# Order of issue inside the slots of a fused FFT-mixing and MLP kernel, and first weight sums in earlier tiles

## The chip, the cores and the metric

One Trainium2 chip, one core of it. The metric is the device time in microseconds of one execution of the whole kernel: a LayerNorm, a 2-D FFT filter with its inverse and a residual, then a LayerNorm, a two-layer MLP with relu and a second residual, all in one program.

The names of engines in the profile: PE is the matrix engine (PEld its weight loads, which overlap its matmuls), DVE the vector engine, ACT the scalar engine, POOL the GpSimd engine, SP the engine whose queue issues the DMAs. PSUM is the memory into which PE writes; POOL cannot reach it.

## The reference

```python
def _A_ref(x, w_r, w_i):
    B, S, D = x.shape
    X = jnp.fft.rfft2(x, axes=(-2, -1)) * (w_r + 1j * w_i)
    return jnp.fft.irfft2(X, s=(S, D), axes=(-2, -1))

def _B_ref(x, w1, w2):
    h = jnp.maximum(jnp.einsum("bsd,df->bsf", x, w1), 0)
    return jnp.einsum("bsf,fd->bsd", h, w2)

h = x + _A_ref(layernorm(x), w_r, w_i)       # x: 1 x 2048 x 576
out = h + _B_ref(layernorm(h), w1, w2)       # w1: 576 x 4608, w2: 4608 x 576
```

All data are float32. The output is `out`.

## The kernel before

**Stages.** The forward transform (L296 on) and the middle of the filter (L340 on) are matmuls with constant tables. Then x is loaded a second time (sixteen DMAs, L377) and a loop over `t` (L641) runs the inverse transform in 16 tiles of 128 rows: `inv_d(t)` makes y (its second half by one POOL subtraction, L396), `inv_a(t-1)` one tile later multiplies y and adds it to x, which gives h in the tile `A`. Two tiles behind that follow the statistics of the second LayerNorm (`stat2`), its application by ACT (`norm2`, two tiles of rows at a time, as a generator that is advanced at the end of each turn of the loop) and `project`, which transposes the normalised rows into `T`.

**The MLP** is cut in 18 blocks `s` (nine blocks of 512 hidden columns, for each half of the rows), and each block is two-level: both layers are computed by a seven-product scheme of Strassen's kind with 2 x 2 blocks. That is why sums of blocks appear on all sides: sums of normalised rows (L419 to L422, POOL), sums of w1 blocks (`sums1`, POOL, L480 to L485), sums of w2 blocks (`sums2`, POOL, L501: T1 to T4), sums of hidden blocks (`hsum`, DVE, L520: S1 to S4). Every float32 operand of a matmul is split in a high and a low part: ACT copies it to a rounded type (L161), DVE subtracts the copy from the operand (L467), and three matmuls (high x high, high x low, low x high) replace one. Such pairs are `split1` (w1, four groups 0 to 3 of the tile `WF`), `split2` (w2 blocks) and `form` (hidden blocks, in the buffers that the profile calls HF, G and one of the e tiles).

**Order.** A unit `S` is 14 slots `k` (`slot`, L626). Slot `k` holds the first-layer product `mm1` of block `S` (six or eight matmuls of 512 columns, L543), its evacuation `evac` (copies and relu by ACT; in three of seven slots a DVE addition, L556, and then the relu of its result by ACT, L557), the second-layer product `prod` of block `S-1` (twelve matmuls of 288 columns, L569) with the DVE addition of its PSUM result into `A` (L574), and small tasks: `tasks_old` for block S-1 and `tasks_new` for block S. `form(S-1, k+2)` prepares the hidden operand of the product two slots on. Unit 0 has no second layer and is spread over turns 16 to 22 of the loop over `t`, two slots a turn, among the last tiles' statistics and transposes; units 1 to 17 have both layers; unit 18 has only the second.

Nothing reorders this: each engine runs its instructions in the order in which the program text issues them, and waits on semaphores where an operand or a buffer is not ready. The order written out by hand is thus the order of every queue, SP's and POOL's too.

Buffers that matter here: `WF` exists once, so a group of it is rewritten only after the last first-layer product that reads it; `V2` keeps each w2 block and its sums in place; hidden operands rotate through four buffers, w2 operands through four (`VF`); products with odd number up to 11 share one PSUM tile (`c1`), and each waits for the addition into `A` of the one before; `X` and `Y` are the two PSUM banks of the first layer. The pool `e` has ten buffers, given out in the order in which they come free; the two w1 blocks (`V1`) and their sums (`SW`) take three of them for good.

The order of products and where their operands come from:

```python
PRODS = "P1a P2a P1b P2b P6a P5a P6b P3a P7a P5b P7b P3b P4a P4b"   # slots 0 to 13
# P1: A11 x B11; P2: A12 x B21; P6: S2 x T2; P5: S1 x T1; P3: S4 x B22; P7: S3 x T3; P4: A22 x T4
ORDER = A11, A12, S2, S1, S3, A22, S4     # first layer, slots 0 to 6 and again 7 to 13
```

Group 0 of `WF` holds A11 and A12, group 1 A22, group 2 S1 and S2, group 3 S3 and S4.

Of the kernel before, what the change touches and what calls it, by code (L numbers as in the profile page):

```python
# [18 lines left out]
NT = 16  # L19
# [105 lines left out]
def kernel(ctx: ExitStack, tc: tile.TileContext, x, w_r, w_i, w1, w2, cc2, c1, fb, ib, c3, out):  # L125
    nc = tc.nc
# [26 lines left out]
    def ebuf(shape, dt=F32):  # L153
        e = sb([128, EW], "e", EB, dt, "e")[:, :int(np.prod(shape[1:]))]
        return e.rearrange("p (a b) -> p a b", a=shape[1]) if len(shape) == 3 else e
# [258 lines left out]
    def norm2(t0):  # L414
        z = ebuf([128, 2, D])
        yield from ln_apply(xs, t0, 2, stats.pop(t0), [z[:, i, :] for i in range(2)])
        S = ebuf([128, 4, 256])
        b11, b21, b12, b22 = z[:, 0, :256], z[:, 0, 256:512], z[:, 1, :256], z[:, 1, 256:512]
        nc.gpsimd.tensor_sub(S[:, 0], b12, b11)  # L419
        nc.gpsimd.tensor_sub(S[:, 2], b22, b12)  # L420
        nc.gpsimd.tensor_sub(S[:, 1], b22, S[:, 0])
        nc.gpsimd.tensor_sub(S[:, 3], b21, S[:, 1])  # L422
        Zs[t0 // 2] = z, S

    def project(i, part):
        P, q = i // 4, slice(128 * (i % 4), 128 * (i % 4) + 128)
# [45 lines left out]
        for h in range(2):  # L472
            nc.sync.dma_start(t[64 * h:64 * h + 64, 4], w1[512:576, f])

    def sums1(v, part):
        t, S = V1[v % 2], M["SW"]
        A11, A12, A21, A22 = (t[:, 2 * k:2 * k + 2, 128 * f:128 * f + 128] for f, k in ((0, 0), (0, 1), (1, 0), (1, 1)))
        S1, S2, S3, S4 = (S[:, 2 * i:2 * i + 2] for i in range(4))
        if part == 0:
            nc.gpsimd.tensor_add(S1, A21, A22)  # L480
            nc.gpsimd.tensor_sub(S2, S1, A11)
        else:
            nc.gpsimd.tensor_sub(S3, A11, A21)
            nc.gpsimd.tensor_sub(S4, A12, S2)
            nc.gpsimd.tensor_sub(S[:, 8], t[:, 4, :128], t[:, 4, 128:])  # L485

    def split1(v, g):
        t, S = V1[v % 2], M["SW"]
# [19 lines left out]
    def split2(s, n_):  # L508
        f = vform(s, n_)
        split(f[:, 0], f[:, 1], V2[PLACE.get(n_, n_)])  # L510
# [6 lines left out]
    def hsum(s, n_, j=slice(0, 2)):  # L517
        d, a, b, f = {"S3": ("S3", "A11", "A21", nc.vector.tensor_sub), "S1": ("A21", "A21", "A22", nc.vector.tensor_add),
                      "S2": ("A11", "A21", "A11", nc.vector.tensor_sub), "S4": ("A12", "A12", "A11", nc.vector.tensor_sub)}[n_]
        f(raw(s, d, j), raw(s, a, j), raw(s, b, j))  # L520
# [58 lines left out]
    def tasks_old(s, k):  # L579
        if k == 0:  # L580
            hsum(s, "S1", 0)
            hsum(s, "S2", 1)
        if k == 1:
            hsum(s, "S2", 0)
        if k in (2, 3):
            split2(s, ("T2", "T1")[k - 2])
            hsum(s, "S4", k - 2)
        if k == 5:
            split2(s, "B22")
            split2(s, "T3")  # L590
        if k == 8:
            split2(s, "T4")

    def tasks_new(s, k):
        u, m = divmod(k, 7)
        v = 2 * s + u
        if v and k == 7:
            split1(v, 1)
        if v and k in (1, 7):
            split1(v, 3)  # L600
        if m == 0 and v + 2 < 2 * NS:
            load1(v + 2)
        if v + 1 < 2 * NS:
            if m in (1, 2):
                sums1(v + 1, m - 1)
            if k in (4, 6, 10, 12, 13):
                split1(v + 1, {4: 0, 6: 2, 10: 0, 12: 2, 13: 1}[k])
        if s:
            for kk, n_ in ((4, "B11"), (5, "B22"), (6, "B12"), (9, "B21")):
                if k == kk:  # L610
                    load2(s, n_)
        if k == 9:
            hsum(s, "S3")
        if k == 11:
            split2(s, "B11")
            sums2("T1", "T3", "T2")
        if k == 12:
            hsum(s, "S1", 1)
        if k == 13:
            split2(s, "B21")  # L620
            sums2("T4")
        if s == 8 and u == 1:
            b = ORDER[m][1]
            nc.sync.dma_start(T[:, b].rearrange("p h k n -> p (h k n)").bitcast(F32), Td[b].rearrange("p a i n -> p (a i n)"))

    def slot(S, k):  # L626
        if S < NS:
            mm1(S, *divmod(k, 7))
            evac(S, *divmod(k, 7))
            if k >= 12:  # L630
                form(S, k - 12)
        if S:
            if k < 12:
                form(S - 1, k + 2)
            prod(S - 1, k)
            tasks_old(S - 1, k)
        if S < NS:
            tasks_new(S, k)

    gen = None  # L640
    for t in range(NT + 7):  # L641
        if t < NT:
            inv_d(t)
        if t == NT - 1:
            pools.pop("x").release()
            newpool("mid", "left")
        if t == 8:
            V1.append(ebuf([128, 5, 256]))
            M["SW"] = ebuf([128, 9, 128])
            load1(0)  # L650
        if t == 10:
            sums1(0, 0)
            sums1(0, 1)
        if t == 12:
            split1(0, 0)
            split1(0, 1)
        if t == 14:
            split1(0, 2)
            split1(0, 3)
        if t == 16:  # L660
            V1.append(ebuf([128, 5, 256]))
            load1(1)
            M.update((n_, sb([128, 512], n_, pool="mid")) for n_ in ("s1", "u2", "u3"))
            pools.pop("pd").release()
            newpool("pxy", "left", space=PSUM)
            M["XY"] = [pools["pxy"].tile([128, 512], F32, tag=n_, name=n_, bufs=1) for n_ in "XY"]
            HF.append(sb([128, 2, 2, 256], "HF", 1, F32R, "mid"))
            V2["T2"] = sb([128, 2, 288], "T2", pool="mid")
        if t == 18:
            for h in ("1", "2"):  # L670
                vv = ebuf([128, 2, 576]).rearrange("p a (j d) -> p a j d", j=2)
                for k in range(2):
                    V2["B" + h + "12"[k]] = vv[:, k]
                    load2(0, "B" + h + "12"[k])
        if t == 20:
            VF.append(ebuf([128, 1152], F32R).rearrange("p (a j d) -> p a j d", a=2, j=2))
        if t == 21:
            VF.append(ebuf([128, 1152], F32R).rearrange("p (a j d) -> p a j d", a=2, j=2))
            HF.append(ebuf([128, 1024], F32R).rearrange("p (a j d) -> p a j d", a=2, j=2))
        if t % 2 == 1 and 5 <= t <= NT + 3:  # L680
            gen = norm2(t - 5)
            next(gen)
        if 0 <= t - 3 < NT:
            stat2(t - 3)
        if 0 <= t - 1 < NT:
            inv_a(t - 1)
        if t >= NT:
            slot(0, 2 * (t - NT))
            slot(0, 2 * (t - NT) + 1)
        if t >= 7:  # L690
            project(*divmod(t - 7, 2))
        if gen:
            next(gen, None)
    for _ in range(2):
        VF.append(ebuf([128, 1152], F32R).rearrange("p (a j d) -> p a j d", a=2, j=2))
    G = sb([128, 2, 1024], "G", 1, F32R, "mid").rearrange("p b (a j d) -> p b a j d", a=2, j=2)
# [29 lines left out]
```

## Time and profile before

| | |
|---|---|
| median of 3 runs | 1084.51 us (1083.0 to 1086.38) |
| the profiled execution | 1083.62 us, span of its instructions 1081.8 us |
| PE busy | 1014.2 us, 94% of the span |
| DVE busy | 883.8 us, 82% |
| ACT, POOL busy | 513.0 us, 357.5 us |
| granted PE clock | 0.995 |
| inverse, from its first tile to the first slot of unit 0 | about 117 to 188 us |
| unit 0 | 188 to 227 us |
| units 1 to 17 | 227 to 1048 us |
| unit 18 and the last stores | 1048 to 1082 us |

How to read the lines of the profile. A line of the timeline is: start in us, busy time of the line's instructions, engine, line of the kernel, operation, output <- inputs by the program's names (buffer numbers left out), shape, how many; in square brackets the idle time just before it and what ended it. A line of waits is: who waited, for whom, microseconds in total, times, the longest. The chain of waits is followed back from the last instruction. A helper records under its own line: L161 is every ACT copy, L467 every subtraction of a split, so the tile's name tells which one is meant (`WF` a w1 split; `e<-e,e` with 576 columns a w2 split; `G`, `HF` or `e<-h,e` with 512 columns a form). Matmuls are pipelined, so that their durations overlap: distances between starts say what a matmul costs.

### The profile page before, as it was taken

The numbers are of one execution on the slowest core, as the hardware profiler recorded it, in microseconds if no ns is written. First come the engines' busy times: TensorE is split into PE (matmuls) and PEld (weight loads), VectorE is DVE, ScalarE is ACT, GpSimd is POOL, SyncE is SP. The second block draws the span as 40 slices with busy tenths as digits, with TensorE's granted clock in tenths as the row PEclk, the third lists the DMA queues.
The fourth block names the chain that finished last, engine by engine and source line by source line (L and its number), as shares of the span: only waits on it lengthen the run. The fifth ranks groups of instructions, "written<-read, shape, count | busy, mean of one in ns | idle before, by whom it ended". The sixth has DMA issues, their size and how long they took to land.

```text
span 1081.8 us, 16681 instructions
## 1 busy us (share of the span) xinstructions
PE 1014.2 (94%) x6344; PEld 884.3 (82%) x6344; DVE 883.8 (82%) x1367; ACT 513.0 (47%) x904; POOL 357.5 (33%) x384
## 2 busy tenths in 40 slices
PE   8999987789999999999999999999999999999997
PEld 7788775668898888889898888888888888888886
DVE  7587788668888888888888888888888888888887
ACT  4533244555454544545445444545445454445443
POOL 4200265542423334241423333241432424142320
PEclk9999998999999999999999999999999999999999
DMA  8840800842021222112111834202111211212003
GB/s 240 197 126 4 198 1 9 261 144 69 25 69 36 58 58 61 58 36 68 36 58 50 321 85 114 69 25 69 36 58 58 61 58 36 69 34 60 16 29 88
DMA packets 73935, 85.12 MB, mean 79 GB/s; under 512 B 5248, under 2 KB 69248, under 8 KB 72960
## 3 DMA queue, kind: packets, MB, share of 16 engines
q1 hardware_dynamic: 73856, 84.06, 27.1%
q8 instruction: 50, 0.82, 0.3%
q14 instruction: 29, 0.24, 0.1%
HBM read 71.98 MB, written 12.06 MB: 78 GB/s over the span
## 4 chain that ended last, share of the span: by engine, by line
DVE 59%; PE 12%; ACT 12%; issue 12%; DMA 2%; POOL 2%; DVEq 0%; SPq 0%; ACTq 0%; POOLq 0%
DVE A L574 14%; DVE h L520 10%; DVE e L467 9%; DVE WF L467 8%; PE d L158 7%; DVE h L556 6%; DVE G L467 5%; ACT h L557 4%; ACT G L161 3%; DVE HF L467 3%; PE dd L158 2%; ACT HF L161 2%; ACT e L161 1%; PE d L569 1%; DMA e<-in_B_w_dram 1%
## 5 line engine op out<-in xcount | busy, mean ns | idle before, releaser
L569 PE MATMUL d<-e,G 128*128 128x288 f32 x1512 | 226.3, 296 | 19.3 <-DVE e L467 16.1
L569 PEld LDWEIGHTS d<-e,G 128*128 128x128 f32 x1512 | 212.5, 188 | 38.3 <-DVE e L467 21.3
L557 ACT ACTIVATE h<-h 128x512 f32<-128x512 f32 x108 | 68.3, 632 | 367.4 <-DVE h L556 367.0
L543 PE MATMUL X<-T,WF 128*128 128x512 f32 x864 | 225.9, 397 | 4.4 <-ACT u L161 3.3
L574 DVE TENSOR_TENSOR A<-A,d 128x576 f32<-128x576 f32 x252 | 188.3, 747 | 1.8 <-PE d L569 1.8
L543 PEld LDWEIGHTS X<-T,WF 128*128 128x128 f32 x864 | 155.2, 189 | 32.0 <-ACT u L161 4.0
L543 PE MATMUL Y<-T,WF 128*128 128x512 f32 x648 | 168.3, 395 | 3.8 <-DVE h L556 3.8
L467 DVE TENSOR_TENSOR G<-h,G 128x512 fp32r<-128x512 f32 x126 | 87.6, 695 | 65.3 <-ACT G L161 65.1
L520 DVE TENSOR_TENSOR h<-h,h 128x512 f32<-128x512 f32 (+1 forms) x126 | 137.5, 1102 | 0.0
L543 PEld LDWEIGHTS Y<-T,WF 128*128 128x128 f32 x648 | 115.8, 188 | 24.0 <-DVE h L556 4.5
L569 PE MATMUL d<-e,e 128*128 128x288 f32 x756 | 113.9, 297 | 13.3 <-DVE e L467 9.8
L569 PEld LDWEIGHTS d<-e,e 128*128 128x128 f32 x756 | 105.9, 188 | 24.6 <-DVE e L467 11.9
L467 DVE TENSOR_TENSOR WF<-e,WF 128x640 fp32r<-128x640 f32 (+2 forms) x144 | 121.9, 858 | 3.2 <-ACT WF L161 3.2
L569 PE MATMUL d<-e,HF 128*128 128x288 f32 x756 | 113.0, 296 | 4.8 <-DVE e L467 4.7
L569 PEld LDWEIGHTS d<-e,HF 128*128 128x128 f32 x756 | 106.7, 188 | 12.9 <-DVE e L467 7.7
L480 POOL TENSOR_TENSOR e<-e 128x256 f32<-128x256 f32 x36 | 40.2, 1117 | 218.1 <-DVE WF L467 215.3
L501 POOL TENSOR_TENSOR e<-e 128x576 f32<-128x576 f32 x18 | 32.3, 1796 | 192.8 <-DVE e L467 192.8
L161 ACT ACTIVATE WF<-e 128x640 fp32r<-128x640 f32 (+2 forms) x144 | 90.8, 644 | 0.0
L161 ACT ACTIVATE G<-h 128x512 fp32r<-128x512 f32 x126 | 77.9, 619 | 16.1 <-DVE h L520 14.0
L467 DVE TENSOR_TENSOR e<-e,e 128x576 fp32r<-128x576 f32 x108 | 79.7, 752 | 1.3 <-ACT e L161 1.3
L161 ACT ACTIVATE e<-e 128x576 fp32r<-128x576 f32 x108 | 70.6, 670 | 0.0
L467 DVE TENSOR_TENSOR HF<-h,HF 128x512 fp32r<-128x512 f32 x63 | 44.2, 702 | 31.9 <-ACT HF L161 31.7
(108 smaller groups left out, 1343.5 us busy)
## 6 DMA issues: line engine op xcount, KB each, us to landing
e<-in_B_w_dram SPq DMA_DIRECT2D x72, 288.0 KB, 2.9
e<-in_B_w_dram SPq DMA_DIRECT2D x36, 512.0 KB, 3.8
Td<-h SPq DMA_DIRECT2D x28, 256.0 KB, 3.1
T<-Td SPq DMA_DIRECT2D x7, 1024.0 KB, 10.4
A<-in_A_x_dram SPq DMA_DIRECT2D x16, 288.0 KB, 9.1
e<-in_B_w_dram SPq DMA_DIRECT2D x72, 64.0 KB, 3.5
out_dram<-A SPq DMA_DIRECT2D x32, 144.0 KB, 2.5
X<-in_A_x_dram SPq DMA_DIRECT2D x12, 288.0 KB, 7.6
```

The costliest lines, as they stand in the source:

```text
L158: nc.tensor.matmul(o, l, r, start=start, stop=stop)
L161: nc.scalar.activation(o, i, AF.Copy, **kw)
L467: nc.vector.tensor_sub(l, v, h)
L480: nc.gpsimd.tensor_add(S1, A21, A22)
L501: nc.gpsimd.tensor_sub(d, a, b)
L520: f(raw(s, d, j), raw(s, a, j), raw(s, b, j))
L543: nc.tensor.matmul(o, l, r, start=first and n_ == 0, stop=n_ == len(ops) - 1, skip_group_check=not first)
L556: nc.vector.tensor_add(h, a, Y)
L557: nc.scalar.activation(h, h, AF.Relu)
L569: nc.tensor.matmul(o[:, tt], f[:, l, j, 128 * tt:128 * tt + 128], w[:, r, j], start=first and n_ == 0, stop=n_ == 5, skip_group_check=not ...
L574: nc.vector.tensor_add(xt, xt, o)
```

## The change

In a slot, `form(S-1, k+2)` now comes first, ahead of the first-layer product and its evacuation (and `form(S, k-12)` in slots 12 and 13). Inside the unit, tasks move: the split of T2 from slot 2 to slot 1; the split of B21 from slot 13 to slot 12; the sum T4 from slot 13 to slot 4 of the next unit, and T2's sum ahead of T3's; half of S1 from slot 12 to slot 13; in slots 9 to 13 the hidden sums and w2 splits come ahead of the w1 tasks; the split of w1's group 3 from slot 1 to slot 2; the two parts of the w1 sums from slots 1, 2, 8, 9 to slots 3, 5, 9, 12.

In the inverse, the buffers and loads of the first two w1 blocks move from turns 8 and 16 to turns 0 and 2, the sums of block 0 from turn 10 to turns 0 and 1, those of block 1 from unit 0 to turns 4 and 5, and the splits of block 0 from turns 12 and 14 to turns 2, 3 and 4. The four POOL sums of the normalised rows are no longer part of the generator: a function `sumsx` issues two of them at the end of one turn and two at the end of the next.

```diff
     def norm2(t0):
         z = ebuf([128, 2, D])
         yield from ln_apply(xs, t0, 2, stats.pop(t0), [z[:, i, :] for i in range(2)])
-        S = ebuf([128, 4, 256])
+        Zs[t0 // 2] = z, ebuf([128, 4, 256])
+
+    def sumsx(i, part):
+        z, S = Zs[i]
         b11, b21, b12, b22 = z[:, 0, :256], z[:, 0, 256:512], z[:, 1, :256], z[:, 1, 256:512]
-        nc.gpsimd.tensor_sub(S[:, 0], b12, b11)
-        nc.gpsimd.tensor_sub(S[:, 2], b22, b12)
-        nc.gpsimd.tensor_sub(S[:, 1], b22, S[:, 0])
-        nc.gpsimd.tensor_sub(S[:, 3], b21, S[:, 1])
-        Zs[t0 // 2] = z, S
+        for d, a, b in (((0, b12, b11), (2, b22, b12)), ((1, b22, S[:, 0]), (3, b21, S[:, 1])))[part]:
+            nc.gpsimd.tensor_sub(S[:, d], a, b)
...
-    def sums1(v, part):
+    def sums1(v, part, only=None):
...
+        ops = ((S1, A21, A22), (S2, S1, A11), (S3, A11, A21), (S4, A12, S2), (S[:, 8], t[:, 4, :128], t[:, 4, 128:]))
+        for n_ in ((0, 1), (2, 3, 4))[part] if only is None else [only]:
+            (nc.gpsimd.tensor_sub if n_ else nc.gpsimd.tensor_add)(*ops[n_])
...
         if k == 1:
             hsum(s, "S2", 0)
-        if k in (2, 3):
-            split2(s, ("T2", "T1")[k - 2])
-            hsum(s, "S4", k - 2)
+            split2(s, "T2")
+        if k == 2:
+            hsum(s, "S4", 0)
+        if k == 3:
+            split2(s, "T1")
+            hsum(s, "S4", 1)
+        if k == 4:
+            sums2("T4")
...
     def tasks_new(s, k):
         u, m = divmod(k, 7)
         v = 2 * s + u
+        if k == 9:
+            hsum(s, "S3")
+        if k == 11:
+            split2(s, "B11")
+            sums2("T1", "T2", "T3")
+        if k == 12:
+            split2(s, "B21")
+        if k == 13:
+            hsum(s, "S1", 1)
         if v and k == 7:
             split1(v, 1)
-        if v and k in (1, 7):
+        if v and k in (2, 7):
             split1(v, 3)
...
-            if m in (1, 2):
-                sums1(v + 1, m - 1)
+            if v and k in (3, 5, 9, 12):
+                sums1(v + 1, int(k in (5, 12)))
...
-        if k == 9:
-            hsum(s, "S3")
-        if k == 11:
-            split2(s, "B11")
-            sums2("T1", "T3", "T2")
-        if k == 12:
-            hsum(s, "S1", 1)
-        if k == 13:
-            split2(s, "B21")
-            sums2("T4")
...
     def slot(S, k):
+        if S and k < 12:
+            form(S - 1, k + 2)
         if S < NS:
+            if k >= 12:
+                form(S, k - 12)
             mm1(S, *divmod(k, 7))
             evac(S, *divmod(k, 7))
-            if k >= 12:
-                form(S, k - 12)
         if S:
-            if k < 12:
-                form(S - 1, k + 2)
             prod(S - 1, k)
             tasks_old(S - 1, k)
...
-        if t == 8:
+        if t in (0, 2):
             V1.append(ebuf([128, 5, 256]))
+            load1(t // 2)
+        if t == 0:
             M["SW"] = ebuf([128, 9, 128])
-            load1(0)
-        if t == 10:
-            sums1(0, 0)
-            sums1(0, 1)
-        if t == 12:
-            split1(0, 0)
-            split1(0, 1)
-        if t == 14:
-            split1(0, 2)
-            split1(0, 3)
+        if t in (0, 1, 4, 5):
+            sums1(t // 4, t % 4)
+        if t in (2, 3, 4):
+            for g in ((2,), (3, 0), (1,))[t - 2]:
+                split1(0, g)
         if t == 16:
-            V1.append(ebuf([128, 5, 256]))
-            load1(1)
...
         if gen:
             next(gen, None)
+        if 6 <= t < NT + 6:
+            sumsx(*divmod(t - 6, 2))
```

More of the change, by code (lines that the diff above doesn't have):

```diff
@@ L478, in sums1 @@
         S1, S2, S3, S4 = (S[:, 2 * i:2 * i + 2] for i in range(4))
[L479 to L485, printed above, removed]
+        ops = ((S1, A21, A22), (S2, S1, A11), (S3, A11, A21), (S4, A12, S2), (S[:, 8], t[:, 4, :128], t[:, 4, 128:]))
+        for n_ in ((0, 1), (2, 3, 4))[part] if only is None else [only]:
+            (nc.gpsimd.tensor_sub if n_ else nc.gpsimd.tensor_add)(*ops[n_])
     def split1(v, g):
```

## The prediction

> **What bounds the kernel now.** I read the busy shares by stretch first, then the chain of waits, then one steady unit in the timeline. Columns of a stretch: length, busy time of PE, PE's weight loads, DVE, ACT, POOL, then granted clock, DMA share, GB/s.
>
> ```profile
> 277.10:325.28 48.18, 46.22 (x270) 41.12 (x270) 40.77 (x58) 23.69 (x43) 16.29 (x15) 1.00 0.18 53
> 126.98:183.19 56.21, 47.45 (x267) 38.58 (x265) 48.64 (x100) 23.65 (x38) 33.72 (x57) 0.97 0.06 16
> ```
>
> ```profile
> 614.41 1.84 DVE h L520
> ...
> 662.58 1.84 DVE h L520
> ```
>
> The chain comes back to the same DVE addition every 48.17 us: that is one unit, and there are 17 with both layers in them (S=1 to 17). PE's 46.22 hides the waits, since modelled ends overlap; starts show them:
>
> ```profile
> 566.17 1.56 PE L543 MATMUL X<-T,WF 128*128 128x512 f32 x6
> 567.57 1.75 PE L569 MATMUL d<-e,G 128*128 128x288 f32 x12
> 569.15 1.56 PE L543 MATMUL Y<-T,WF 128*128 128x512 f32 x6
> ...
> 571.01 0.30 PE L569 MATMUL d<-e,G 128*128 128x288 f32 x1
> 572.42 1.73 PE L569 MATMUL d<-e,G 128*128 128x288 f32 x11 [1.12 <-DVE e L467]
> ...
> 579.28 1.83 PE L569 MATMUL d<-e,e 128*128 128x288 f32 x12 [0.29 <-DVE A L574]
> ...
> 583.16 1.73 PE L569 MATMUL d<-e,G 128*128 128x288 f32 x11 [0.53 <-DVE e L467]
> ```
>
> Six first-layer matmuls take 1.40 from start to start (566.17 to 567.57), eight 1.86 (569.15 to 571.01), twelve second-layer ones 1.58. A unit has 100 and 168 of them: 100 x 0.232 + 168 x 0.1325 = 45.46. So 48.18 - 45.46 = 2.72 us per unit are waits, all on DVE: product 1 for the split of B21, product 3 for the sum of product 1, product 4 for the split of T2. The unit's waits say why DVE is late:
>
> ```profile
> DVE G L467 <- ACT G L161: 3.7, 3, 1.3
> DVE e L467 <- ACT e L161: 2.4, 2, 1.2
> DVE HF L467 <- ACT HF L161: 1.2, 1, 1.2
> PE d L569 <- DVE e L467: 1.6, 2, 1.1
> PE d L569 <- DVE A L574: 0.3, 1, 0.3
> ```
>
> Six times DVE adds u+Y (L556), ACT does the relu and only then the copy of the form, and DVE, whose next work is that form's subtraction, stands 1.22 us: 7.3 us. 40.8 busy + 7.3 = 48.1: DVE is full.
>
> **The change: forms first.** The form's copy and subtraction now stand ahead of the addition, so nothing on DVE follows a relu directly. The six waits go (-7.3 us of DVE per unit). If that were all, PE would stream at 45.46. But POOL moves too, and it costs DVE time:
>
> ```profile
> 562.36 0.75 DVE L574 TENSOR_TENSOR A<-A,d 128x576 f32<-128x576 f32 x1
> 563.03 0.75 DVE L467 TENSOR_TENSOR e<-e,e 128x576 fp32r<-128x576 f32 x1
> 563.70 0.69 DVE L467 TENSOR_TENSOR G<-h,G 128x512 fp32r<-128x512 f32 x1
> 564.30 0.75 DVE L574 TENSOR_TENSOR A<-A,d 128x576 f32<-128x576 f32 x1
> 564.96 1.25 DVE L467 TENSOR_TENSOR WF<-e,WF 128x512 fp32r<-128x512 f32 x1
> 566.14 1.92 DVE L520 TENSOR_TENSOR h<-h,h 128x512 f32<-128x512 f32 x1
> 567.98 0.67 DVE L556 TENSOR_TENSOR h<-u,Y 128x512 f32<-128x512 f32 x1
> ...
> 579.65 0.82 DVE L467 TENSOR_TENSOR WF<-e,WF 128x640 fp32r<-128x640 f32 x1
> 580.49 0.69 DVE L467 TENSOR_TENSOR G<-h,G 128x512 fp32r<-128x512 f32 x1
> ```
>
> ```profile
> 563.86 1.81 POOL L501 TENSOR_TENSOR e<-e 128x576 f32<-128x576 f32 x1 [10.29 <-DVE e L467]
> 565.75 1.76 POOL L501 TENSOR_TENSOR e<-e,e 128x576 f32<-128x576 f32 x1
> ...
> 580.55 1.25 POOL L483 TENSOR_TENSOR e<-e 128x256 f32<-128x256 f32 x1 [3.99 <-DVE WF L467]
> ```
>
> Starts give the free pitches: 0.66 for A, 0.67 for a w2 split, 0.60 for a 512-wide one. Against POOL they take turns: POOL's first T ends 565.67, and the WF subtraction from 564.96 hands on only at 566.14, 0.47 later; the second T ends 567.51, and the hidden sum from 566.14 hands on at 567.98, again 0.47. POOL in turn ends 1.30 after the DVE operation that held it (566.21 to 567.51), a w1 sum 0.62 after (581.18 to 581.80). A, which reads PSUM, keeps 0.66 beside POOL.
>
> The Trainium skill, page "SBUF — State Buffer", section "Who interferes with whom", calls this an exclusive lock for DVE instructions with two SBUF inputs against GpSimd ones that read SBUF. The trace agrees (0.47 after 565.67 and after 567.51). By that rule the new POOL order costs PE a wait; without it the sum would be the first rival's.
>
> POOL's queue after product 12 is now T1, T2, T3, then the second part of the w1 sums (slot 12), its first part (slot 3), T4 (slot 4). Their inputs are there, so POOL runs them in one go; before, T4 and the sums waited on splits. I lay DVE's order against that, with 0 where product 12 hands PE on. PE would hand on product 13 at 3.45, 0 at 6.43, 1 at 9.88, 2 at 12.86, 3 at 16.31 (1.39 or 1.86 for the first layer, 1.59 for the product). T1 starts behind form 0's subtraction and ends at 0.4; T2, free, takes 1.4 (1.30 and a start) and ends at 1.9. DVE, with the moment at which it hands on ("sum k" adds product k into A, L574; "addition" is L556; "half of S" an L520 sum of hidden blocks):
> sum 12 0.86; B21's split, held by T2, 1.9 + 0.54 = 2.43 (T3 then ends 2.51 + 1.30 = 3.81); WF group 2, held by T3, 4.28 (first w1 sum 4.96); form 1 5.43 (second 6.11); addition 13 6.03; sum 13 6.69 (third, short, meanwhile); half of S1 7.29 (fourth 7.97); group 1 8.31 (fifth 8.99); form 2 9.46 (T4 10.84); sum 0 10.12; the other half of S1, held by T4, 11.31; half of S2 11.91; form 3 12.51; addition 1 13.11; sum 1 13.77; half of S2 14.37; T2's split, whose copy follows the relu of addition 1, 15.19; form 4 15.79; sum 2 16.45; half of S4 17.05; WF group 3 (now slot 2, was slot 1; 0.74 free, from 579.65 on without the short sum's hold) 17.79, its result 0.08 later. Then:
> - Product 1 needs B21 at 6.43 + 1.86 = 8.29, has it at 2.5: its wait goes. Product 3 needs sum 1 at 14.7, has it at 13.9. Product 4 has T2 in time. So all three old waits go.
> - New: the third matmul of slot 4 needs group 3's low half at 16.31 + 0.46 = 16.77 and gets it at 17.93: **1.16 us of wait**. From there DVE regains PE by slot 9 and the unit closes.
> Unit: 45.46 + 1.16 = 46.6, a gain of 1.55 to 1.6; over 17 units -27. Bounds: no wait, -2.72 each; two sums changing turns puts it 0.7 later, and half as much again, -0.8 each: -14 to -46.
>
> **First tiles.** The load of the first w1 block moves from tile 8 to tile 0 on SP, behind the sixteen x loads; its POOL sums from tile 10 to tiles 0 and 1, ahead of the y subtraction (L396) of tile 1.
>
> ```profile
> 106.54 13.04 SPq L170 DMA_DIRECT2D A<-in_A_x_dram  x16
> ```
>
> ```profile
> A<-in_A_x_dram SPq DMA_DIRECT2D x16, 288.0 KB, 9.1
> ```
>
> ```profile
> 107.00:128.00 21.00, 19.66 (x168) 16.34 (x165) 12.71 (x26) 4.13 (x8) 2.65 (x3) 1.00 0.97 225
> ```
>
> ```profile
> 123.40 1.13 PE L158 MATMUL dd<-e,cc 128*128 128x288 f32 x4
> ...
> 167.10 3.58 PE L158 MATMUL d<-e,X 128*128 128x290 f32 x12
> ```
>
> ```profile
> 126.98 0.46 DVE L393 TENSOR_TENSOR e<-e,d 128x288 f32<-128x288 f32 x1 [0.77 <-ACT e L161]
> ...
> 166.08 1.78 DVE L467 TENSOR_TENSOR WF<-e,WF 128x640 fp32r<-128x640 f32 x2
> ...
> 171.24 0.46 DVE L393 TENSOR_TENSOR e<-e,d 128x288 f32<-128x288 f32 x1 [0.65 <-POOL e L419]
> ...
> 178.63 1.92 DVE L467 TENSOR_TENSOR WF<-e,WF 128x512 fp32r<-128x512 f32 x2
> ...
> 192.73 0.69 DVE L556 TENSOR_TENSOR h<-s,Y 128x512 f32<-128x512 f32 x1 [1.96 <-PE Y L543]
> ```
>
> The DMA engines are 97% busy to 128; the last x load, issued at 119, lands 9.1 later. 512 KB behind it at 225 GB/s need 2.3, and the landing some 0.7: about 131. POOL stands until then, adds twice (0.7 each, the free time of a 256-wide sum: 1.25 at 580.55 less the 0.55 in which DVE's form held it) and makes tile 1's y by 133.2. PE, whose order has tile 1's second half in the matmuls at 123.40, stands behind it from 124.0 to 133.3. After 3.7 idle, tile 13's matmuls took 3.58 at 167.10; I take that for tile 3, so DVE's L393 of tile 3 comes at 138.0, 11.0 after 126.98. From there DVE sets the pace (48.64 busy of 56.21). Splits of groups 3, 0 and 1 now lie in tiles 3 and 4 (0.74, 0.74, 0.47: +1.95); those at 166.08 and 178.63 go (-1.7, -1.85) and so does the 0.65 at 171.24. PE, no longer late, removes the 1.96 at 192.73. Sum: 11.0 + 1.95 - 3.55 - 0.65 - 1.96 = +6.8; take **+6.5**, bounds +2 (the load at 129, the clock up) to +10 (nothing regained).
>
> The page "DMA: Bandwidth & Descriptors" of the Trainium skill, section "Two DMAs through the same engine are not ordered", lets descriptors of one queue start in order, though they finish out of it; it speaks against the change. In the trace the x loads' 9.1 fit a line that is waited in; no row shows one overtaken.
>
> **The small edits.** The four normalised-tile sums (sumsx) go out in pairs a tile apart: PE's waits for POOL there shrink, but DVE sets the pace, so I count 0, and up to -3 if DVE were not the cover. SP issues nothing urgent behind the early loads: 0. ACT's form copies stand ahead of the X copies that release a bank; by the walk the copy after slot 4's X ends 0.8 before slot 5 needs it: 0, and 0.5 a unit if ACT is later. The last unit:
>
> ```profile
> 1051.49 1.73 PE L569 MATMUL d<-e,G 128*128 128x288 f32 x11 [1.59 <-DVE e L467]
> ```
>
> B21's wait of 1.59 goes there; with fewer POOL sums I take -2 (0 to -3).
>
> **Sum.** The profiled execution took 1083.6 (its span 1081.8); the median shown is 1084.5, 0.1% above. 1083.6 - 27 + 6.5 - 2 = 1061; I say **1060**.
>
> **Rivals.**
> - *Group 3 is in time*, PE streams at 45.46: 17 x 2.72 = 46, 1083.6 - 46 + 6.5 - 2 = **1042**. For: the wait hangs on 1.16 out of a walk of 18 us. Against: DVE and POOL collide nine times in it.
> - *The early load costs nothing* (lands among the x loads): the +6.5 becomes about -3.5, **1051**. Against: 97% DMA share to 128.
> - *Collisions eat the gain, slower*: place, slots 12 to 3; if each of five w1 sums holds DVE some 0.4 longer, group 3 comes 2 later, the wait is 3.2, the unit 48.6: +8 + 6.5 - 2, **1096**. It decides once the new wait is over 2.45. Against: the turns at 564.96 and 566.14 are regular.
> - *It doesn't do what it says*: a late addition holds ACT, form copies stay late, DVE stays full at 48.1 and only the first tiles differ: **1088**. Against: a form's copy needs nothing of its own slot.
>
> **How the numbers follow.** Forecast 0.53, in time 0.23, load free 0.12, collisions 0.07, nothing 0.05. The likeliest one's own range is 1047 (a wait of 0.5, first tiles +3) to 1074 (a wait of 1.9); reaching to the first rival's 1042 and part of the slower ones gives 1040 to 1078. Over 0.3% (3.3 us; less can't be told from no change) faster: 0.53 + 0.23 + 0.12 = 0.88; the last two cases split into 0.04 same and 0.08 slower.
>
> **What would show it.** Right: the chain's period at 46.6; no DVE wait on ACT for G, HF or e forms; one PE wait per unit, for DVE WF, ahead of an X group; nine POOL operations in one run; POOL's first w1 sum waiting on DMA to about 131 and PE idle some 9 us from 124, at a lower clock after. Wrong: a period of 45.5 or 48; PE still waiting for e L467; no idle PE at 124.

## The result, and the profile after

The changed kernel takes **1077.69 us** (median of 4 runs, 1076.89 to 1078.19), the kernel before 1085.24 on the same chip (4 runs, 1083.00 to 1086.38). The ratio is 0.9932, interval 0.9913 to 0.9951: faster by 7.5 us, where 24 were forecast. The time lies in the range given, but at its upper end, and the forecast of the gain was three times too large.

The head of the profile's page, of the kernel after:

```profile
span 1075.4 us, 16681 instructions
...
PE 1011.2 (94%) x6344; PEld 887.4 (83%) x6344; DVE 921.2 (86%) x1367; ACT 514.9 (48%) x904; POOL 368.4 (34%) x384
```

DVE is busy 37 us longer for the same 1367 instructions, POOL 11 us longer for the same 384: the same work, held up more. Where the time went shows in the start of the first first-layer matmul of a unit. Timeline of PE before, units 0, 1, 2 and 17 (start, length, engine, line, operation; L543 is the first layer):

```profile
187.74 1.04 PE L543 MATMUL X<-T,WF 128*128 128x512 f32 x1
...
226.73 0.50 PE L543 MATMUL X<-T,WF 128*128 128x512 f32 x1 [1.13 <-ACT h L552]
...
277.06 0.63 PE L543 MATMUL X<-T,WF 128*128 128x512 f32 x2
...
999.82 0.40 PE L543 MATMUL X<-T,WF 128*128 128x512 f32 x1
```

and the same four after (lines have moved by four: the first layer is L539 now, the product L565, the addition into A L570, the addition u+Y L552, the hidden sums L516, T1 to T4 L497, the w1 sums L481):

```profile
197.40 1.04 PE L539 MATMUL X<-T,WF 128*128 128x512 f32 x1
...
240.46 0.78 PE L539 MATMUL X<-T,WF 128*128 128x512 f32 x1
...
287.49 0.40 PE L539 MATMUL X<-T,WF 128*128 128x512 f32 x1
...
996.33 0.40 PE L539 MATMUL X<-T,WF 128*128 128x512 f32 x1
```

PE's last matmul ends at 1077.08 before and at 1070.67 after. The differences make a budget beside the prediction's terms (its 17 units divided as 1 + 15 + 1):

| stretch | before | after | measured | forecast |
|---|---|---|---|---|
| to the start of unit 0 | 187.74 | 197.40 | +9.66 | +6.5 |
| unit 0 | 38.99 | 43.06 | +4.07 | 0 |
| unit 1 | 50.33 | 47.03 | -3.30 | -1.6 |
| units 2 to 16 | 722.76 | 708.84 | -13.92 | -23.7 |
| start of unit 17 to PE's end | 77.26 | 74.35 | -2.91 | -3.6 |
| sum | | | **-6.4** | **-22.4** |

**A steady unit** after takes 47.26 on average (48.18 before). PE's timeline in one of them has two waits, where one was forecast:

```profile
581.13 1.65 PE L539 MATMUL Y<-T,WF 128*128 128x512 f32 x6 [0.77 <-DVE h L552]
...
585.85 1.19 PE L539 MATMUL X<-T,WF 128*128 128x512 f32 x4 [0.56 <-DVE WF L467]
```

Starts against the pitch of 0.232 make them 0.93 and 0.72, and the next matmul comes 0.11 late each time. The second is the forecast wait for group 3 in slot 4. The first is the Y group of slot 3, which waits until addition 1 (the DVE addition u+Y of slot 1) has emptied the PSUM bank Y. The three old waits (for `e L467` twice, for `A`) are gone, and so are the six of DVE; what DVE still waits for in this unit:

```profile
DVE A L570 <- PE d L565: 2.3, 3, 1.1
DVE WF L467 <- ACT WF L161: 1.2, 2, 0.7
DVE e L467 <- ACT e L161: 0.9, 2, 0.6
```

No hidden form is in it (the two `e` are 576 wide, splits of w2). DVE and POOL over the stretch that sets both PE waits:

```profile
568.22 1.68 DVE L467 TENSOR_TENSOR e<-e,e 128x576 fp32r<-128x576 f32 x1
569.82 1.92 DVE L467 TENSOR_TENSOR WF<-e,WF 128x512 fp32r<-128x512 f32 x1
571.66 1.23 DVE L467 TENSOR_TENSOR G<-h,G 128x512 fp32r<-128x512 f32 x1
...
574.07 1.09 DVE L516 TENSOR_TENSOR h<-h,h 128x512 f32<-128x512 f32 x1
575.08 1.09 DVE L467 TENSOR_TENSOR WF<-e,WF 128x384 fp32r<-128x384 f32 x1
576.09 1.92 DVE L467 TENSOR_TENSOR HF<-h,HF 128x512 fp32r<-128x512 f32 x1
...
580.40 0.67 DVE L552 TENSOR_TENSOR h<-s,Y 128x512 f32<-128x512 f32 x1
...
584.98 0.82 DVE L467 TENSOR_TENSOR WF<-e,WF 128x640 fp32r<-128x640 f32 x1
```

```profile
565.95 1.82 POOL L497 TENSOR_TENSOR e<-e 128x576 f32<-128x576 f32 x1 [12.69 <-DVE e L467]
...
574.68 1.07 POOL L481 TENSOR_TENSOR e<-e,e 128x256 f32<-128x256 f32 x1
575.72 1.75 POOL L497 TENSOR_TENSOR e<-e,T 128x576 f32<-128x576 f32 x1
```

POOL's nine operations do run in one go, 565.95 to 577.47. Six DVE operations in it last 0.4 to 1.24 longer than alone. The one that the prediction had in another order is the last: T4 got its turn ahead of form 2's subtraction (576.09, 1.92 instead of 0.68), and addition 1 (580.40) handed on at 581.00, 0.54 later than the walk had it.

**First tiles.** PE, POOL and DVE after (L393 is each tile's first subtraction on DVE: tiles 3, 7 and 15):

```profile
131.53 0.72 POOL L481 TENSOR_TENSOR e<-e 128x256 f32<-128x256 f32 x1 [10.80 <-DMA e<-in_B_w_dram]
...
133.77 1.32 PE L158 MATMUL dd<-e,cc 128*128 128x288 f32 x2 [9.77 <-POOL e L396]
...
134.88 3.93 PE L158 MATMUL d<-e,X 128*128 128x290 f32 x12
...
139.30 0.46 DVE L393 TENSOR_TENSOR e<-e,d 128x288 f32<-128x288 f32 x1 [3.41 <-ACT e L161]
...
154.19 0.45 DVE L393 TENSOR_TENSOR e<-e,d 128x288 f32<-128x288 f32 x1
...
194.26 0.45 DVE L393 TENSOR_TENSOR e<-e,d 128x288 f32<-128x288 f32 x1
```

This is the forecast picture, with POOL standing on the load to 131.5 and PE idle for 9.77. And **unit 0** has a wait that nobody had forecast:

```profile
233.48 1.42 POOL L497 TENSOR_TENSOR e<-e 128x576 f32<-128x576 f32 x1 [2.17 <-DVE e L467]
...
237.69 2.38 POOL L423 TENSOR_TENSOR e<-e,e 128x256 f32<-128x256 f32 x2
```

```profile
238.92 1.89 PE L434 MATMUL d<-ident,e 128*128 128x128 f32 x6 [4.39 <-POOL e L423]
```

The second pair of the last normalised rows' sums (L423, `sumsx(7, 1)`) stands on POOL behind T1, T2 and T3, which slot 11 issues earlier in the same turn of the loop; the transposes of `project(7, 1)` (L434) need it, and PE stands 4.39 us. That wait costs twice: behind it PE runs unit 1's first matmuls at a lower granted clock (0.57 on average from 240.46 to 245.00, the row is in the last section): the six of the first X group start 0.43 apart instead of 0.23, and by starts the stretch takes 1.85 longer. The rest of unit 1 has neither the Y wait nor the group 3 wait.

### The profile page after: what moved, and what is told of

It is laid out like the page before. It is cut to its first block, busy times and chain, and to the rows that moved or that the text cites. A ratio compares the mean times of both kernels' runs of the same rounds, so it can differ in the third digit from the quotient of the medians.

```text
span 1075.4 us, 16681 instructions
## 1 busy us (share of the span) xinstructions
PE 1011.2 (94%) x6344; PEld 887.4 (83%) x6344; DVE 921.2 (86%) x1367; ACT 514.9 (48%) x904; POOL 368.4 (34%) x384
## 4 chain that ended last, share of the span: by engine, by line
PE 56%; DVE 30%; ACT 7%; issue 3%; DMA 2%; POOL 2%; SPq 1%; POOLq 0%; DVEq 0%; ACTq 0%
PE d L565 22%; PE X L539 15%; PE Y L539 9%; PE d L158 6%; DVE WF L467 6%; DVE e L467 5%; DVE A L570 4%; DVE G L467 3%; DVE h L516 3%; PE dd L158 2%; DVE HF L467 2%; DVE h L552 2%; ACT e L161 1%; ACT WF L161 1%; DVE st L220 1%
## 5 line engine op out<-in xcount | busy, mean ns | idle before, releaser
L539 PE MATMUL X<-T,WF 128*128 128x512 f32 x864 | 230.4, 399 | 12.1 <-DVE WF L467 8.8
L570 DVE TENSOR_TENSOR A<-A,d 128x576 f32<-128x576 f32 x252 | 188.2, 747 | 41.5 <-PE d L565 41.3
L565 PEld LDWEIGHTS d<-e,G 128*128 128x128 f32 x1512 | 213.7, 188 | 11.8 <-issue 1.4
L565 PE MATMUL d<-e,G 128*128 128x288 f32 x1512 | 221.2, 295 | 1.2 <-DVE A L570 1.0
L481 POOL TENSOR_TENSOR e<-e 128x256 f32<-128x256 f32 (+1 forms) x108 | 98.2, 916 | 300.0 <-DVE WF L467 289.2
L539 PEld LDWEIGHTS X<-T,WF 128*128 128x128 f32 x864 | 154.8, 190 | 44.5 <-DVE WF L467 15.8
L539 PE MATMUL Y<-T,WF 128*128 128x512 f32 x648 | 169.0, 396 | 15.5 <-DVE h L552 15.5
L467 DVE TENSOR_TENSOR WF<-e,WF 128x640 fp32r<-128x640 f32 (+2 forms) x144 | 142.4, 1000 | 32.5 <-ACT WF L161 32.5
L539 PEld LDWEIGHTS Y<-T,WF 128*128 128x128 f32 x648 | 115.4, 188 | 38.6 <-DVE h L552 19.5
L565 PEld LDWEIGHTS d<-e,e 128*128 128x128 f32 x756 | 106.9, 188 | 7.4 <-issue 1.8
L565 PE MATMUL d<-e,e 128*128 128x288 f32 x756 | 110.9, 295 | 1.8 <-DVE A L570 1.6
L565 PEld LDWEIGHTS d<-e,HF 128*128 128x128 f32 x756 | 107.7, 189 | 5.3
L565 PE MATMUL d<-e,HF 128*128 128x288 f32 x756 | 111.2, 296 | 0.0
L497 POOL TENSOR_TENSOR e<-e 128x576 f32<-128x576 f32 x18 | 32.3, 1796 | 229.6 <-DVE e L467 216.9
L467 DVE TENSOR_TENSOR e<-e,e 128x576 fp32r<-128x576 f32 x108 | 96.6, 908 | 15.7 <-ACT e L161 14.4
L516 DVE TENSOR_TENSOR h<-h,h 128x512 f32<-128x512 f32 (+1 forms) x126 | 109.8, 882 | 0.0
L467 DVE TENSOR_TENSOR G<-h,G 128x512 fp32r<-128x512 f32 x126 | 103.6, 823 | 0.1
L481 POOL TENSOR_TENSOR e<-e,e 128x256 f32<-128x256 f32 x72 | 82.0, 1139 | 2.8
L161 ACT ACTIVATE u<-X 128x512 f32<-128x512 f32 x72 | 42.5, 590 | 82.4 <-PE X L539 82.3
```

The costliest lines, as they stand in the source:

```text
L161: nc.scalar.activation(o, i, AF.Copy, **kw)
L467: nc.vector.tensor_sub(l, v, h)
L481: (nc.gpsimd.tensor_sub if n_ else nc.gpsimd.tensor_add)(*ops[n_])
L497: nc.gpsimd.tensor_sub(d, a, b)
L539: nc.tensor.matmul(o, l, r, start=first and n_ == 0, stop=n_ == len(ops) - 1, skip_group_check=not first)
L565: nc.tensor.matmul(o[:, tt], f[:, l, j, 128 * tt:128 * tt + 128], w[:, r, j], start=first and n_ == 0, stop=n_ == 5, skip_group_check=not ...
```

## The experiments

The theory after the result: the change is two changes. Forms first gains; the moved work costs most of that again, at four places (the first sums behind the load, the last normalised sums behind T3, T4 in POOL's run, group 3 a slot late). The rival: the new order as such is worse (DVE is held by POOL wherever the work is put), or the forms bring little.

What all kernels took, by the same marks as above ("unit" is the mean of units 2 to 16; the three groups of runs had 1085.22, 1084.74 and 1084.66 us for the kernel before):

| kernel | start of unit 0 | unit 0 | unit 1 | unit | from unit 17 | time, us |
|---|---|---|---|---|---|---|
| before | 187.74 | 38.99 | 50.33 | 48.18 | 77.26 | 1085.2 |
| after | 197.40 | 43.06 | 47.03 | 47.26 | 74.35 | 1077.69 |
| forms only | 187.74 | 39.45 | 48.65 | 45.87 | 75.00 | 1047.78 |
| forms undone | 197.98 | 42.94 | 50.29 | 48.95 | 77.43 | 1110.01 |
| first sums later | 186.98 | 42.80 | 47.17 | 47.29 | 74.51 | 1066.22 |
| last pair first | 197.69 | 39.28 | 49.64 | 47.27 | 74.53 | 1075.91 |
| T4 late | 197.67 | 43.45 | 46.68 | 46.07 | 73.29 | 1057.82 |
| no w1 sums | 197.46 | 43.11 | 47.09 | 45.77 | 73.04 | 1055.03 |
| group 3 in slot 1 | 197.13 | 43.45 | 46.64 | 46.27 | 73.51 | 1062.10 |
| before, improved | 187.98 | 39.63 | 48.10 | 45.43 | 74.56 | 1039.52 |
| after, repaired | 186.23 | 41.03 | 48.57 | 45.33 | 72.41 | 1034.13 |

Not every difference in the column "unit" is a wait. By starts, PE's waits in a steady unit (with the late matmul behind each) are 2.71 before, 1.87 after, 0.70 with the forms only, 3.6 with the forms undone, 0.60 with T4 late, 0.60 without the w1 sums, 1.12 with group 3 in slot 1, and none in "before, improved". What is left of the unit is about 45.45 or about 45.16, as the first-layer matmuls follow each other in 0.233 or in 0.227 (last section): before, after, T4 late and "before, improved" ran mostly in the longer pitch, forms only, no w1 sums and group 3 in slot 1 in the shorter one. So up to 0.3 us of a difference between two units is pitch. The prices below overlap too, and can't be added.

### Forms only, on the kernel before

```diff
 def slot(S, k):
+    if S and k < 12:
+        form(S - 1, k + 2)
     if S < NS:
+        if k >= 12:
+            form(S, k - 12)
         mm1(S, *divmod(k, 7))
         evac(S, *divmod(k, 7))
-        if k >= 12:
-            form(S, k - 12)
     if S:
-        if k < 12:
-            form(S - 1, k + 2)
         prod(S - 1, k)
```

> The kernel before, with only slot() changed: forms ahead of the first-layer product and its evacuation; every task, sum and load where it was. Theory 'the forms' place carries the gain, and the moved tasks cost it again by putting POOL's nine operations in one run': the six DVE waits on ACT go, group 3 (slot 1) and B21 (slot 13, ready about 7.3 us after product 12, needed at 8.3) are in time, the unit falls from 48.18 to 45.5 to 45.9, seventeen of them: 1040 to 1047 us. Rival 'the moved splits of B21 and T2 carry the gain': the waits for B21 and T2 stay in part, the unit at 47 to 48: 1065 to 1083 us.

Measured: 1047.78 us, 0.9653 (0.9628 to 0.9679); faster than the whole change by 30 us, and just above the 1040 to 1047 of the theory. The unit is 45.87. PE's three old waits are gone, and the one wait that there is now is a Y group's again, for addition 1 (L556 in this kernel):

```profile
560.92 1.63 PE L543 MATMUL Y<-T,WF 128*128 128x512 f32 x6 [0.43 <-DVE h L556]
```

So this wait doesn't come from the moved work. It is next behind the removed ones in either order of tasks.

### Forms undone, in the kernel after

The same lines of `slot` turned back, all moved work kept.

> The changed kernel with slot() as before: forms behind the evacuation again; tasks, sums, tiles as changed. Theory 'forms carry the gain': the six DVE waits of 1.22 us come back, DVE is full, the unit is 48.2 or longer: 1090 to 1110 us. Rival 'the moved splits carry the gain': the unit stays near 47.3: 1077 to 1081 us.

Measured: 1110.01 us, 1.0222 (1.0200 to 1.0244), the unit 48.95. DVE's six waits are back (waits of one unit: us in total, times, longest):

```profile
DVE HF L467 <- ACT HF L161: 2.5, 2, 1.3
DVE e L467 <- ACT e L161: 2.4, 2, 1.2
DVE G L467 <- ACT G L161: 2.4, 2, 1.2
...
PE X L539 <- DVE WF L467: 1.4, 1, 1.4
```

With the two edits apart, the four kernels make a square: the unit is 48.18 with neither, 45.87 with the forms alone, 48.95 with the moved work alone, 47.26 with both. Forms first takes off 2.31, or 1.69 beside the moved work; the moved work adds 0.77, or 1.39 beside the forms. The gain wasn't lost in the mechanism that was meant to bring it.

### T4 later

```diff
 def tasks_old(s, k):
-        if k == 4:
-            sums2("T4")
+        if k == 6:
+            sums2("T4")
```

> The changed kernel with one POOL subtraction, T4, moved from slot 4 to slot 6, so that it no longer follows the w1 sums in one run. Theory (the collisions of POOL's run make addition 1 and WF group 3 late): the run ends with the last w1 sum, form 2's subtraction no longer stands behind T4 for 1.1 us, addition 1 comes some 0.6 before the Y group of slot 3 needs it and that wait of 0.93 goes; group 3 comes 0.6 earlier and its wait falls to 0.1 to 0.5. Unit 47.25 to 45.9-46.3, time 1077.7 - 17 x 1.15 = 1057 to 1062. Rival (DVE's own order, not T4, sets these two moments): unit 47.2, 1077.

Measured: 1057.82 us, 0.9744 (0.9719 to 0.9768); the unit is 46.07, the Y wait is gone, group 3's is down to 0.50 by starts:

```profile
569.50 0.68 DVE L467 TENSOR_TENSOR HF<-h,HF 128x512 fp32r<-128x512 f32 x1
...
572.57 0.68 DVE L552 TENSOR_TENSOR h<-s,Y 128x512 f32<-128x512 f32 x1
```

```profile
578.02 1.20 PE L539 MATMUL X<-T,WF 128*128 128x512 f32 x4 [0.34 <-DVE WF L467]
```

Form 2 takes 0.68 where it took 1.92: that one turn of 1.24 was worth 1.2 us of every unit (of PE's waits, 1.87 to 0.60). T4 itself costs nothing in slot 6.

### Without the w1 sums

```diff
-            if v and k in (3, 5, 9, 12):
+            if s == 0 and v and k in (3, 5, 9, 12):
```

> The changed kernel without the twenty-odd us of weight sums of the first layer from unit 1 on: POOL does not make them, and the splits take what lies in their buffer (this part of the computation is left out). The order on DVE, ACT, PE and SP stays. T4 stays, and now runs right behind T3. Theory (POOL's w1 sums hold DVE and so bring the two new waits): the five holds of 0.2 to 0.6 go, addition 1 and group 3 come about 1.5 earlier, both waits go, unit 45.5 to 45.7, time 1077.7 - 17 x 1.65 = 1048 to 1051. Rival (the order on DVE alone costs the two waits): unit 47.2, 1077. In between: T4 alone still holds one form and leaves one of the two waits, unit 46.3, 1062.

Measured: 1055.03 us, 0.9719 (0.9698 to 0.9740), the unit 45.77. The time lies between the two forecasts (1048 to 1051, and 1062), and the unit between the theory's 45.5 to 45.7 and the in-between case's 46.3, nearer the first; one wait of 0.50 by starts is left, a Y group's:

```profile
563.18 1.91 DVE L467 TENSOR_TENSOR G<-h,G 128x512 fp32r<-128x512 f32 x1
565.01 0.68 DVE L552 TENSOR_TENSOR h<-u,Y 128x512 f32<-128x512 f32 x1
```

```profile
565.74 1.63 PE L539 MATMUL Y<-T,WF 128*128 128x512 f32 x6 [0.34 <-DVE h L552]
```

T4, now right behind T3, holds another form (G, 1.91 instead of 0.68), and so another addition is late, that of slot 13, on which the Y group of slot 1 waits. Without the w1 sums the unit is 1.49 shorter, 1.27 of it waits. That DVE's own order sets the two waits is ruled out.

### Group 3 in slot 1

```diff
-        if v and k in (2, 7):
+        if v and k in (1, 7):
             split1(v, 3)
```

> The changed kernel with the split of WF group 3 back in slot 1, as the kernel before has it; all else as changed. Theory of two separate waits: the wait of 0.72 ahead of the X group of slot 4 goes, but the split now stands ahead of no less work than it did, so addition 1 is unchanged (the split is issued after it in slot 1) and the Y group of slot 3 still waits 0.93; T2's split, issued ahead of it, is in time. Unit 47.25 - 0.83 = 46.4, time 1063. Rival (the two waits are one delay: PE, let go earlier by the one, meets the next late DVE result, sum 2 or the split of T2 or half of S4): unit 47.0 to 47.2, 1074 to 1077.

Measured: 1062.10 us, 0.9784 (0.9763 to 0.9805), the unit 46.27. The X wait is gone, the Y wait is still there (1.01 by starts, 0.93 in the change):

```profile
575.16 1.63 PE L539 MATMUL Y<-T,WF 128*128 128x512 f32 x6 [0.85 <-DVE h L552]
```

The two waits are separate: one can be taken away without the other. Moving this split from slot 1 to slot 2 cost 0.99 a unit, 0.75 of it waits (1.87 to 1.12).

### First sums later

The two w1 loads stay in tiles 0 and 2; their POOL sums move from tiles 0, 1, 4 and 5 to tiles 4, 5, 8 and 9, the splits from tiles 2 to 4 to tiles 6 to 8.

```diff
-        if t in (0, 1, 4, 5):
-            sums1(t // 4, t % 4)
-        if t in (2, 3, 4):
-            for g in ((2,), (3, 0), (1,))[t - 2]:
+        if t in (4, 5, 8, 9):
+            sums1((t - 4) // 4, t % 4)
+        if t in (6, 7, 8):
+            for g in ((2,), (3, 0), (1,))[t - 6]:
                 split1(0, g)
```

> The changed kernel, with the two early loads and the early buffers kept, but the w1 sums of blocks 0 and 1 four tiles later (tiles 4, 5, 8, 9) and the splits of block 0 at tiles 6, 7, 8. Theory 'POOL stands on the load': the 9.8 us for which PE was idle from 124 us go, and the low clock after it; tile 3's first DVE subtraction (L393) comes back from 139.3 to about 127, the splits still cost about 2 us of DVE, unit 0 begins 11 to 13 us earlier (at 185 to 187 instead of 197.4), the units stay at 47.3: 1065 us. Rival 'three of the ten e buffers are taken too early': the first tiles stay as late as they are, unit 0 begins at 195 or later: 1075 to 1078 us.

Measured: 1066.22 us, 0.9817 (0.9796 to 0.9839): 11.5 less than the change. PE's idle time of 9.77 is gone, and tile 3 is back at its old moment:

```profile
127.32 0.45 DVE L393 TENSOR_TENSOR e<-e,d 128x288 f32<-128x288 f32 x1 [0.83 <-ACT e L161]
```

Unit 0 starts at 186.98 instead of 197.40, and from there on the two kernels are alike. POOL's wait for the load is thus what the first tiles lose; the early buffers, which this run keeps, are not. But the start is only 0.76 ahead of the kernel before, so the other moves in the first tiles bring next to nothing.

### Last pair first

```diff
+        if t == 21:
+            sumsx(7, 1)
         if t >= NT:
             slot(0, 2 * (t - NT))
...
-        if 6 <= t < NT + 6:
+        if 6 <= t < NT + 5:
             sumsx(*divmod(t - 6, 2))
```

> The changed kernel with one call moved: in turn 21 the last pair of sums of normalised rows (sumsx(7, 1)) is issued ahead of slots 10 and 11, so ahead of the three T sums on POOL. Theory 'the last transposes wait for these sums behind the T sums' (PE idle 4.39 us at 234.5 for POOL L423): that wait goes, unit 1 begins about 4 us earlier: 1073.5 us. Rival 'it lies beside another wait': under 1.5 us gained, 1076 to 1078 us.

Measured: 1075.91 us, 0.9907 (0.9884 to 0.9930). That is 1.8 below the change's median, in another group of runs, and the two intervals overlap: closer to the rival (1076 to 1078) than to the 1073.5. The 4.39 are gone and unit 0 is 3.78 shorter, but unit 1 is 2.61 longer:

```profile
236.97 1.66 PE L539 MATMUL X<-T,WF 128*128 128x512 f32 x6 [1.24 <-ACT h L548]
...
242.18 1.65 PE L539 MATMUL Y<-T,WF 128*128 128x512 f32 x6 [1.96 <-DVE h L552]
```

PE meets the next late addition, which DVE reaches at 241.44 behind three subtractions of 1.60, 1.22 and 1.21 us that alternate with T3 and the w1 sums. With the 4.39 the low clock behind it is gone as well (1.00 from 236.97 to 242.00), yet unit 1 now has four waits of 2.11, 0.54, 0.31 and 0.72 by starts where the change had none. Over the two units 1.17 of the 3.78 is left.

### The kernel before, improved

Forms first; one half of hidden sum S2 from slot 0 to slot 1; the first load in tile 0, its sums one by one in tiles 4 to 8, its splits in tiles 5, 7, 9 and 10.

```diff
         if k == 0:
             hsum(s, "S1", 0)
-            hsum(s, "S2", 1)
         if k == 1:
+            hsum(s, "S2", 1)
             hsum(s, "S2", 0)
...
+        if t in (4, 5, 6, 7, 8):
+            sums1(0, None, t - 4)
+        if t in (5, 7, 9, 10):
+            split1(0, {5: 0, 7: 2, 9: 1, 10: 3}[t])
```

> The kernel before with the forms first in a slot, its own order of all other work in a unit but for one DVE half sum of S2 moved from slot 0 to slot 1 behind addition 1, and with the first w1 load in tile 0, its five POOL sums one by one in tiles 4 to 8 and its four splits in tiles 5, 7, 9 and 10. Theory: with forms alone the unit is 45.86, of which 0.59 is the Y group of slot 3 waiting for addition 1; a DVE half sum of 0.6 less ahead of it takes that wait away, unit 45.4 to 45.5, 17 x 0.4 = 7; the spread first sums take away PE's 3.70 wait and some of the 1.33 of the first tiles, unit 0 starts 1 to 3 earlier. Time 1047.8 - 7 - 2 = 1039 (1037 to 1042). Rival (the half sum only moves to the next late result, and the first tiles are set by DVE): 1046 to 1048.

Measured: 1039.52 us, 0.9578 (0.9555 to 0.9601), as forecast in sum, but not term by term. The unit is 45.43 without a wait, 0.44 less than with the forms alone: the wait of 0.70 is gone, and 0.25 came back as the longer pitch. The first tiles gained nothing (unit 0 starts at 187.98, 0.24 later than before): PE's wait of 3.69 in them goes, others come up in other tiles.

### The kernel after, repaired

Four placements altered at once: first sums later, last pair first, T4 late and group 3 in slot 1, each as above.

> The changed kernel with four placements altered at once, all else of the change kept: first w1 sums in tiles 4, 5, 8 and 9 and their splits in tiles 6 to 8; the last pair of normalised-tile sums ahead of slot 11; T4 in slot 6; group 3's split in slot 1. Theory (these placements, and not the moved work as such, cost the change its gain, and each lies in a stretch of its own): unit 0 starts at 187 as with the later sums alone, takes 39.3 as with the earlier pair alone, unit 1 48.8, the fifteen units after it 45.5 each as neither wait is left, and 73.0 from the start of unit 17 to the end of PE: 187 + 39.3 + 48.8 + 682.5 + 73 = 1030.6, and 4.7 to the end of the span and 2 around it give 1037 (1035 to 1041). Rival (the moved order is worse as such: with both waits gone PE meets the next late DVE result): units of 46.0 to 46.3, 1045 to 1050.

Measured: 1034.13 us, 0.9536 (0.9508 to 0.9564): the fastest of all, 43.6 below the change as made and just below the 1035 to 1041 of the theory. Unit 0 took 41.03 instead of 39.3, for a reason that isn't shown; all other stretches came out at or below what was expected. The busy times of a stretch of one unit's length (length, PE, its weight loads, DVE, ACT, POOL, granted clock, DMA share, GB/s):

```profile
537.00:582.45 45.45, 45.45 (x272) 41.40 (x272) 42.40 (x58) 24.22 (x45) 17.25 (x14) 1.00 0.25 76
```

PE is busy in every moment of it. The moved work is no worse as such: altering four placements of it, all at once, gave 43.6 us (some of it the shorter pitch).

## Why the prediction was right or wrong

The miss is 16.0 us (-6.4 measured by the marks, -22.4 forecast): 9.8 in the steady units, 3.2 in the first tiles, 4.1 in unit 0 and 0.7 from unit 17 on, less 1.7 in unit 1.

**Right: DVE was full, and the forms stood behind relus.** The six waits are gone after, and back when the forms alone are turned back, at the same 7.3 us. The rival by which the change does nothing is out. All three old PE waits went, as claimed. The floor, 45.46, is what the two last kernels reach (45.43, and 45.33 with part of it in the shorter pitch).

**Wrong, the step "New": the list of what PE needs was not complete.** It laid the walk of DVE's work against the products' operands and the weight groups, not against the banks X and Y. The Y group of slot 3 can start only after addition 1. By the prediction's own walk addition 1 hands on at 13.11, and that group is due at 12.86: a wait of 0.25 was there to be read, and it wasn't looked for. It measured 0.93, since addition 1 handed on at 13.65 (0.54 later, by the turns of the next paragraph) and PE started 0.13 behind it. (The walk's last step, from 17.79 and 0.08 to 17.93, holds 0.06 that it doesn't name.)

**Mis-sized in the same step: two turns.** The walk let form 2 go ahead of T4. In the trace T4 was issued while DVE's group 1 split still ran, got the next turn and held form 2 until the end of it. The prediction named a price for two sums changing turns (0.7 later), but put it in the bounds. The Trainium skill, page "SBUF — State Buffer", section "Who interferes with whom", says that the order of issue decides which of DVE and GpSimd blocks. T4 is in the record from 575.72, form 2 from 576.09, and the trace agrees; in the runs the turn was worth 1.2 us a unit.

**Right in kind, the group 3 wait:** forecast 1.16, measured 0.72 (PE had already stood 0.93 for Y, so came later), and 0.99 a unit when the split goes back to slot 1, 0.75 of it waits. The rival "group 3 is in time" had no case without that. Together the two waits made the unit 47.26 instead of 46.6, 0.66 each for the fifteen steady units: 9.8 us of the miss. Unit 1 took back 1.7: it was priced by a steady unit's waits, but its own had been longer before (50.33), and after it has none of them, only the 1.85 of its low clock.

**Mis-sized, "First tiles", +6.5 against +9.66.** The mechanism (POOL behind the load, to 131 by forecast, 131.53 by trace) is shown by the run with the sums later, 10.4 us at the start of unit 0. Two rows of the kernel before give the pieces:

```profile
138.83 0.45 DVE L393 TENSOR_TENSOR e<-e,d 128x288 f32<-128x288 f32 x1
...
183.19 0.44 DVE L393 TENSOR_TENSOR e<-e,d 128x288 f32<-128x288 f32 x1
```

Tile 3 came 12.32 late (139.30 against 126.98) instead of 11.0; of the 1.3 more, the load is 0.5 (131.53 for 131; the 0.7 that the forecast put for the landing stood on no row), and the twelve matmuls behind the idle time are 0.35 (3.93 for 3.58). Tiles 3 to 7 took 14.89 instead of 11.85, +3.04 where the splits were priced at 1.95. Tiles 7 to 15 took 40.07 instead of 44.36, -4.29, against -4.20 forecast. The rest to unit 0 gave back 1.41 instead of 1.96. That makes +9.66. The rival "the early load costs nothing" would have been wrong too: with the load's wait gone, unit 0 starts 0.76 earlier, not 3.5.

**Wrong, "The small edits": the pairs of normalised sums, counted 0.** The step weighed them in the tiles, where DVE covers them. The last pair isn't in the tiles: its queue on POOL has T1 to T3 ahead of it, and the 4.39 that PE stands there make unit 0 longer by 4.07. The step didn't name the queue that the moved instruction now stands behind. Its net worth is less than the wait, some 1.2 us, as the last-pair run showed: with the wait gone, PE meets late DVE results at the start of unit 1.

**Right in size, in part by luck: the last unit.** From the start of unit 17 PE needs 2.91 less; a steady unit's 0.92 in it leaves 2.0, as forecast. The 1.59 for B21 is gone, as claimed. But another split's wait of 1.09 is gone too, and the waits for two sums have grown, from 1.08 to 1.63 and from 0.23 to 1.03; none of that was in the forecast, and it nearly cancels. Before, then after:

```profile
1055.89 1.83 PE L569 MATMUL d<-e,e 128*128 128x288 f32 x12 [1.08 <-DVE A L574]
```

```profile
1050.19 1.83 PE L565 MATMUL d<-e,e 128*128 128x288 f32 x12 [1.63 <-DVE A L570]
```

## What to carry to other kernels

When an engine in the middle of a hand-ordered pipeline is freed, list everything that the fed engine needs in each slot, the banks it writes among them, and lay all of it against the walk: here the wait next in line was a bank's, in either order of tasks. Keep an in-order engine from running all its spare work in one go beside an engine that it shares turns with, since one operation on the wrong side of a turn can hold the chain in every round (here 1.24, and 1.2 us of each unit). When an instruction moves, name the queue that it stands behind in its new place. And test the parts of a change apart: here one part was worth 37 us, and the other, badly placed at four spots, took 30 of them back.

## What the runs showed of the hardware

**Turns.** In these traces a POOL operation that is issued while DVE still holds the turn gets the next one, even with DVE's next operation right behind (both engines' operands in SBUF): form 2 took 1.92 us so (576.09) and 0.68 without T4 (569.50 in the kernel with T4 late).

**Clock.** Behind 9.77 us of idle PE the granted clock was 0.62 on average for the next 6.23 us, and PE busy all the time. The 4.39 of idle time at 234.5 were followed by 0.57 for 4.54 us. Columns as in the row of the repaired kernel above; kernel after:

```profile
124.00:133.77 9.77, 0.00 (x1) 0.01 (x1) 1.38 (x4) 0.63 (x1) 2.16 (x4) 0.72 0.88 225
133.77:140.00 6.23, 6.23 (x20) 5.09 (x21) 2.59 (x4) 1.15 (x3) 2.82 (x4) 0.62 0.00 0
...
240.46:245.00 4.54, 4.54 (x18) 3.96 (x17) 4.15 (x6) 1.57 (x4) 4.46 (x6) 0.57 0.00 0
```

**Two pitches.** With PE never waiting, the first-layer matmuls follow each other in one of two times at the same granted clock of 1.00. The chain of the repaired kernel, two X groups of six matmuls:

```profile
560.77 1.37 PE X L539 x6
...
615.80 1.40 PE X L539 x6
```

That is 0.228 or 0.233 each, in stretches, and the units of this kernel repeat as 45.16, 45.37 and 45.47. What chooses between the two stays open; no run was made for it. It is worth 0.3 us a unit at most, which is as much as 5 us over seventeen units: a difference of that size between two of these kernels can be pitch and not waits.
